# A Mamba-2 scan with top-1 experts on one core: sized second pass, transposes by DMA, and a respaced recurrence

## The chip, the cores and the metric

The kernel runs on one core of one Trainium2 chip. The metric is the device time of one execution in microseconds; the median of three runs of the kernel before is 324.8 us (323.02 to 328.04). The profile is of one execution with a span of 323.2 us from first to last instruction. Engines are called TensorE (PE, its weight loads PEld), VectorE (DVE), ScalarE (ACT), GpSimd (POOL) and SyncE (SP).

## The reference

Two parts follow one another. The first is a chunked state-space scan over 4 batches, 8 heads, 768 positions, head size 32 and state size 16:

```python
for c in range(nc):                                   # chunks of 32 in the reference
    cum = np.cumsum(log(clip(a, 1e-6, 1))[..., chunk], axis=-1)
    M = (C @ B.T) * exp(cum_i - cum_j) * causal
    y = M @ x + (C @ state) * exp(cum)
    state = exp(sum) * state + sum_j(exp(cum_last - cum_j) * B_j x_j)
```

The result, laid out as 3072 tokens of 256 numbers, goes through eight experts, one per token:

```python
logits = x @ w_gate                     # 3072 x 8
e = argmax(logits); gate = max(softmax(logits))
out[t] = gate[t] * (relu(x[t] @ w1[e]) @ w2[e])       # w1 256x1024, w2 1024x256
```

All is float32. The inputs are drawn with a fixed seed.

## The kernel before

**Recurrence.** The scan uses chunks of 64. A step `n` (24 of them, `NT`) is one chunk of two batches, a tile of 128 tokens. The loop over `n` is a pipeline of three: step `n` gets its decays (`a_rows` on TensorE, `decay`, a scan on VectorE), its scores (`scores`) and their weighing (`weigh`); step `k = n-1` gets its own state (`own`), the faded state (`fade`, `state`) and `y`; step `j = n-2` is turned into token rows with the eight logits (`rows`, a matmul with `turn` and a ScalarE copy). `scaled_B` and the decayed C (`ctd`, in `decay_in`) are made on GpSimd. The order on each engine is the order in which the Python calls stand: the schedule is written by hand.

**Routing.** Rows are collected in groups (`RGS`, five of 6, 6, 4, 4 and 4 tiles). For a group, `choose` finds the best expert and the one-hot (VectorE), `rank_pe` counts with small matmuls how many tokens of the same expert stand ahead, `rank` makes of it a row number in the table `x_hbm`, `gate_sum` and `gate` the softmax weight, which is stored in the row beside the token number. `place` scatters 128 rows by an indirect DMA from GpSimd, two calls a step. Each expert has a region in `x_hbm`; `empty` fills its first 448 rows with zeros and the token number N, which the last scatter drops. The first three groups (`GA`) may be read by the first pass; tokens of later groups stand behind row 256 (`CA`).

**Experts.** The first pass takes 256 rows of each expert, the second 192 more (`CB`): one full tile of 128 and a half tile of 64, two experts' halves sharing one tile (`m_half`). `m_load` reads rows, `xT_of` and `m_xT` transpose them on TensorE with VectorE copying the result, `m_h` makes the hidden layer (8 blocks of 128, ScalarE's ReLU evicting), `m_y` the output, `put` scales by the gate and scatters to `out`. The order is one hidden layer ahead: hidden of unit `u`, output of unit `u-1`. If any expert had more than 448 tokens, `general` would run; it doesn't with these inputs.

**Loads.** SyncE's queue issues them in program order. `load(g)` brings CT, BT, B and x for four steps into three rotating buffers; the weights of four experts (`EW`) are loaded in the loop, one matrix every second step from step 8, the rest during the first experts. The last eight tiles are placed in a row during the first pass, in front of the reads of the second.

Of the kernel before, what the change touches and what calls it, by code (L numbers as in the profile page):

```python
# [11 lines left out]
I32 = mybir.dt.int32  # L12
AX = mybir.AxisListType.X
# [7 lines left out]
CH = 64  # L21
# [5 lines left out]
RGS = [6, 6, 4, 4, 4]  # L27
GA = 3
# [4 lines left out]
GATE, TOK = DM + E, DM + E + 1  # L33
W = DM + E + 2
# [5 lines left out]
EW = 4  # L40
# [3 lines left out]
def ssd_then_moe(ctx, tc, x, ad_in, az_in, B, BT, CT, w_gate, w1, w2, out):  # L44
# [11 lines left out]
    ld = att.enter_context(tc.tile_pool(name="ld", bufs=3))  # L56
# [18 lines left out]
    zrows = sm.tile([112, CAP // 112, W], FP32, name="zrows")  # L75
# [13 lines left out]
    nk = route.tile([128, 2 * E + 1], I32, name="nk")  # L89
    spare = route.tile([1, 1], FP32, name="spare")  # L90

    def wake():

        z = sm.tile([128, 512], BF16, name="wake")
        nc.vector.memset(z, 0.0)
        p = ps.tile([128, 512], FP32, name="wake_ps", tag="rows", bufs=1)
        for _ in range(13):
            nc.tensor.matmul(p, lhsT=z[:, 0:128], rhs=z, start=True, stop=True)
# [22 lines left out]
    def late_consts(hs):  # L121
        for c in (slice(0, CG), slice(CG, NC)):
            nc.scalar.copy(hsel[:, c], bc(hs[:, c, :, None], list(hsel[:, c].shape)))
            if c.start == 0:
                nc.scalar.copy(selx[:, 2:2 * NC], bc(sel[:, 2:2 * NC, None], [128, 2 * NC - 2, CH]))

    def route_consts():
        nc.scalar.copy(turn[:, 0:128], ident)
        nc.scalar.copy(turn[:, 128 + 2 * E:], ident)
        nc.gpsimd.memset(cnt[:, 0, :], 0.0)  # L130
        nc.gpsimd.memset(cnt[:, GA + 1, :], 0.0)

        nc.gpsimd.memset(zrows, 0.0)
        none_i = sm.tile([112, CAP // 112], I32, name="none_i")
        nc.gpsimd.iota(none_i, pattern=[[0, CAP // 112]], base=N, channel_multiplier=0)
        nc.gpsimd.tensor_copy(zrows[:, :, TOK].bitcast(I32), none_i)
        nc.gpsimd.memset(Tmat, 1.0)
        nc.gpsimd.affine_select(out=Tmat, in_=Tmat, pattern=[[1, 128]], base=-1, channel_multiplier=-1,
                                compare_op=ALU.is_ge, fill=0.0)
        nc.gpsimd.memset(ones_bf, 1.0)  # L140
        iota_i = sm.tile([128, E], I32, name="iota_i")
        nc.gpsimd.iota(iota_i, pattern=[[1, E]], base=0, channel_multiplier=0)
        nc.gpsimd.tensor_scalar(out=rev_e, in0=iota_i, scalar1=-1.0, scalar2=float(E), op0=ALU.mult, op1=ALU.add)
        nc.gpsimd.tensor_scalar(out=base_f, in0=iota_i, scalar1=float(NR), scalar2=None, op0=ALU.mult)
        nc.gpsimd.tensor_scalar(out=base_e, in0=iota_i[0:1], scalar1=float(NR), scalar2=None, op0=ALU.mult)
        for s in range(2):
            nc.gpsimd.iota(tok_i[64 * s:64 * s + 64, :].rearrange("p (b c) -> p b c", b=NP),
                           pattern=[[2 * S, NP], [CH, NC]], base=S * s, channel_multiplier=1)

    def empty(e):  # L150
        nc.sync.dma_start(out=x_hbm[e * NR:e * NR + CAP, :].rearrange("(p c) w -> p c w", c=CAP // 112), in_=zrows)
# [15 lines left out]
    def split_az(eng, p, t):  # L167

        z = azp[p]
        f = t.rearrange("p h i -> p (h i)")  # L170

        def first():
            clip(eng, t)
            eng.memset(t[:, :, 0:1], 0.0)
        return [first,
                lambda: eng.tensor_copy(z, f),
                lambda: eng.tensor_tensor(out=f, in0=f, in1=z, op=ALU.subtract),
                lambda: eng.tensor_copy(z[32:64], f[32:64]),
                lambda: eng.tensor_copy(z[64:96], f[64:96]),
                lambda: eng.tensor_tensor(out=f[64:96], in0=f[64:96], in1=z[64:96], op=ALU.subtract),  # L180
                lambda: eng.tensor_copy(z[64:96], f[64:96])]

    def load(g):
        p, c0 = divmod(g * CG, NC)
        r = gr[g]
        T = CG * 128
        sl = slice(c0 * 128, c0 * 128 + T)
        r["CT"] = ld.tile([128, T], FP32, name="ct")
        nc.sync.dma_start(out=r["CT"], in_=CT[p, :, sl])
        r["BT"] = ld.tile([128, T], FP32, name="bt")  # L190
        nc.sync.dma_start(out=r["BT"], in_=BT[p, :, sl])
        r["B"] = ld.tile([128, CG, 128], FP32, name="bn")
        nc.sync.dma_start(out=r["B"], in_=B[p, :, c0:c0 + CG, :])
        r["x"] = ld.tile([128, CG, DM], FP32, name="xn")
        nc.sync.dma_start(out=r["x"], in_=x[p, :, c0:c0 + CG, :])

    def load_w(i):
        e, u = divmod(i, 2)
        nc.sync.dma_start(out=w_sb[e][u], in_=(w1, w2)[u][e])

    def masks(g):

        m = wk.tile([128, CG, 2, 2, CH], FP32, name="ctm")
        for u in range(2):
            nc.scalar.mul(m[:, :, :, u, :], gr[g]["CT"].rearrange("p (c s i) -> p c s i", c=CG, s=2), par[:, u:u + 1])
        gr[g]["ctm"] = m
# [6 lines left out]
    def decay_rows(t):  # L213

        d1 = sm.tile([128, NP * 2, CH], FP32, name="d1")
        nc.gpsimd.memset(d1, 0.0)
        clip(nc.gpsimd, t)
        nc.gpsimd.tensor_copy(d1[:, :, 0:1], t[:, :, 0:1])
        nc.gpsimd.memset(t[:, :, 0:1], 0.0)
        f = sm.tile([128, NP * 128], FP32, name="adf")  # L220
        nc.vector.tensor_tensor_scan(out=f, data0=t.rearrange("p h i -> p (h i)"),
                                     data1=d1.rearrange("p h i -> p (h i)"), initial=0.0, op0=ALU.mult, op1=ALU.add)
        return f

    def decay_split(f, ii):
        for i in ii:
            nc.gpsimd.tensor_copy(adp[i], f)
            if i < 2:
                nc.gpsimd.tensor_tensor(out=f, in0=f, in1=adp[i], op=ALU.subtract)
# [7 lines left out]
    def decay_in(ns, bank):  # L237
        for i, n in enumerate(ns):
            p, c = divmod(n, NC)
            for u in range(3):  # L240
                nc.tensor.matmul(bank[:, i], lhsT=hsel[:, c].rearrange("p h m -> p (h m)"),  # L241
                                 rhs=adp[u][:, 128 * p:128 * p + 128], start=(u == 0), stop=(u == 2),
                                 skip_group_check=True)
        for i, n in enumerate(ns):
            s = st[n]
            s["dec"] = wk.tile([128, 128], FP32, name="dec", bufs=4)
            nc.scalar.copy(out=s["dec"], in_=bank[:, i])  # L247
            s["ctd"] = wk.tile([128, 128], FP32, name="ctd", bufs=4)
# [3 lines left out]
    def a_rows(n):  # L252
        p, c = divmod(n, NC)
        t = ps.tile([128, 512], FP32, name="abc", bufs=2)
        nc.tensor.matmul(t, lhsT=selx[:, 2 * c:2 * c + 2].rearrange("p c j -> p (c j)"), rhs=azp[p],
# [11 lines left out]
    def scaled_B(n):  # L267
        nc.gpsimd.tensor_tensor(out=bs[n % 2], in0=gr[n // CG]["B"][:, n % CG].rearrange("p (h m) -> p h m", h=8),
                                in1=bc(st[n]["L"][:, :, CH - 1:CH], [128, 8, NS]), op=ALU.mult)

    def scores(n):
        c = n % CG
        g = ps.tile([128, 2, 512], FP32, name="g", bufs=1)
        for s in range(2):
            for t in range(2):
                for v in range(2):
                    r = slice(64 * t + 32 * v, 64 * t + 32 * v + 32)
                    o = c * 128 + s * CH
                    nc.tensor.matmul(g[64 * t:64 * t + 64, v, 128 * s:128 * s + 128],  # L279
# [15 lines left out]
    def own(k):  # L295
# [5 lines left out]
        for s in range(2):  # L301
            for t in range(2):
                for v in range(2):
                    r = slice(64 * t, 64 * t + 64)
                    h = 4 * s + 2 * v
                    nc.tensor.matmul(A[32 * (2 * t + v):32 * (2 * t + v) + 32, 0, 64 * s:64 * s + 64],  # L306
# [30 lines left out]
    def y(k):  # L337
# [3 lines left out]
        if inter:  # L341
            for s in range(2):
                for t in range(2):
                    for v in range(2):
                        r = slice(64 * t + 32 * v, 64 * t + 32 * v + 32)
                        o = s * CH
                        nc.tensor.matmul(p[64 * v:64 * v + 64, t, s * CH:s * CH + CH], lhsT=carry[k][r, s],  # L347
                                         rhs=st[k]["ctd"][r, o:o + CH], start=(s == 0), stop=False,
                                         skip_group_check=True)
        for s in range(2):  # L350
            for q in range(4):
                for t in range(2):
                    r = slice(64 * t, 64 * t + 64)
                    o = (4 * s + q) * D
                    nc.tensor.matmul(p[D * q:D * q + D, t, s * CH:s * CH + CH], lhsT=xk[r, o:o + D],  # L355
# [9 lines left out]
    def rows(k):  # L365

        p = ps.tile([128, DM + E], FP32, name="rows_ps", tag="rows", bufs=1)
        for t in range(KT):
            nc.tensor.matmul(p[:, 128 * t:128 * t + HB], lhsT=st[k]["yT"][:, t], rhs=turn[:, HB * t:HB * t + HB],  # L369
# [9 lines left out]
    def choose(g):  # L379
        n = RGS[g]  # L380
        sl = slice(R0[g], R0[g] + n)
# [6 lines left out]
        ex = route.tile([128, RG, E], FP32, name="ex")[:, 0:n]  # L388
        nc.scalar.activation(ex, sub, func=ACT.Exp)
# [3 lines left out]
                                       op0=ALU.is_equal, op1=ALU.mult)  # L393
        m2 = route.tile([128, RG], FP32, name="m2")[:, 0:n]
        nc.vector.tensor_reduce(m2, eq, axis=AX, op=ALU.max)
        nc.vector.tensor_tensor(out=oh_all[:, sl, :], in0=eq, in1=bc(m2[:, :, None], sh), op=ALU.is_equal)
        cs = route.tile([128, E], FP32, name="cs")
        nc.vector.tensor_reduce(cs, oh_all[:, sl, :].rearrange("p k e -> p e k"), axis=AX, op=ALU.add)
        nc.gpsimd.tensor_tensor(out=cnt[:, ci(g) + 1, :], in0=cnt[:, ci(g), :], in1=cs, op=ALU.add)
        rt_ex[g] = ex  # L400

    rt_ex, rt_se = {}, {}

    def gate_sum(g):
        n = RGS[g]
        se = rt_se[g] = route.tile([128, RG], FP32, name="se", bufs=2)[:, 0:n]
        nc.vector.tensor_reduce(se, rt_ex[g], axis=AX, op=ALU.add)
        nc.gpsimd.tensor_scalar_add(se, se, 1e-9)
        nc.gpsimd.tensor_copy(rt[g][:, :, TOK].bitcast(I32), tok_i[:, R0[g]:R0[g] + n])

    def gate(g):
        nc.vector.reciprocal(rt[g][:, :, GATE], rt_se[g])
# [3 lines left out]
    def rank_pe(g, p):  # L416
# [4 lines left out]
        nc.tensor.matmul(q, lhsT=ones_bf, rhs=bc(cnt[:, ci(g):ci(g) + 1, :], [128, n, E]), start=True, stop=False,  # L421
# [100 lines left out]
    def m_h(u, mo, pp, between):  # L522
# [3 lines left out]
        for f in range(FT):  # L526
            p = up(ex[u]["xT"][:, :, 0:n], w_sb[e][0], f, n, pp)
            nc.scalar.activation(ex[u]["hT"][:, f, 0:n], p, func=ACT.Relu)  # L528
            if f == FT // 2:
                between()  # L530
# [247 lines left out]
```

## Time and profile before

| what | us |
|---|---|
| median of three runs | 324.8 |
| span of the profiled run | 323.2 |
| TensorE busy | 289.2 (89%) |
| ScalarE busy | 105.0 (32%) |
| GpSimd busy | 92.1 (29%) |
| VectorE busy | 79.1 (24%) |
| first expert matmul starts | 112.49 |
| last matmul of TensorE ends | 316.6 |
| DMA moved | 39.93 MB |

How to read it: the busy shares are means over two very different halves. Up to 112 us the small matmuls of the recurrence alternate with work of all other engines; from there the expert matmuls run. The strip of 40 slices (8 us each) shows it:

```profile
PE   6679688788687899999999996999999999999991
PEld 2457466666565788888888885889999799798870
DVE  6937555753546522000000000010010010000000
ACT  5635334342243333223231412132233123332310
POOL 5874457235453100202111282102111101211121
PEclk9979787985689899999999999999999999999997
DMA  7969386936435693071720134100001101100000
```

Each digit is the busy share of a slice in tenths; PEclk is the clock that TensorE was granted.

### The profile page before, as it was taken

To read this page: it belongs to the slowest core of one execution; us is meant where nothing else is said; L and a number is where in the kernel's file an instruction comes from. 1 tells how busy PE (TensorE), PEld (TensorE's weight loads), DVE (VectorE), ACT (ScalarE), POOL (GpSimd) and SP (SyncE) were. 2 spreads that over 40 slices of the span, in tenths; PEclk is the share of its full clock that TensorE was granted. 3 is DMA by queue.
4 is the path that set the end of the run, shared out by engine and by line. 5 is a ranking of instruction groups with operands and counts; after the bars stand their busy time and mean duration, and the time that the engine had idled before them with its cause. 6 is when DMAs were issued, how large, how long until landed. Compare 5 with 4: busy or idle time off the path is not lost.

```text
span 323.2 us, 7506 instructions
## 1 busy us (share of the span) xinstructions
PE 289.2 (89%) x3150; PEld 241.2 (75%) x3172; DVE 79.1 (24%) x198; ACT 105.0 (32%) x292; POOL 92.1 (29%) x191
## 2 busy tenths in 40 slices
PE   6679688788687899999999996999999999999991
PEld 2457466666565788888888885889999799798870
DVE  6937555753546522000000000010010010000000
ACT  5635334342243333223231412132233123332310
POOL 5874457235453100202111282102111101211121
PEclk9979787985689899999999999999999999999997
DMA  7969386936435693071720134100001101100000
GB/s 229 355 201 306 130 308 200 315 130 199 113 103 163 257 370 153 31 291 38 290 68 16 50 118 131 33 13 34 0 32 47 36 0 53 43 18 2 19 16 31
DMA packets 13867, 39.93 MB, mean 124 GB/s; under 512 B 2299, under 2 KB 6014, under 8 KB 11776
## 3 DMA queue, kind: packets, MB, share of 16 engines
q1 hardware_dynamic: 11328, 32.94, 30.0%
q0 software_dynamic: 2496, 6.42, 5.5%
q8 instruction: 27, 0.44, 0.6%
q14 instruction: 16, 0.13, 0.1%
HBM read 29.12 MB, written 10.75 MB: 123 GB/s over the span
## 4 chain that ended last, share of the span: by engine, by line
PE 68%; issue 17%; POOL 5%; ACT 3%; DVE 3%; another core or an unknown queue 2%; DMA 1%; POOLq 0%; ACTq 0%
PE h_ps L519 23%; PE y_ps L546 20%; PE rows_ps L369 5%; PE g L279 5%; PE y L355 4%; POOL out_dram L535 3%; PE y L347 3%; PE A L306 2%; PE xT_ps L499 2%; PE A L241 1%; PE y_ps L556 1%; ACT rows L372 1%; DMA az<-in_az_dram 1%; POOL ctd L250 1%
## 5 line engine op out<-in xcount | busy, mean ns | idle before, releaser
L519 PE MATMUL h_ps<-xT,w 128*128 128x256 f32 (+1 forms) x512 | 102.6, 354 | 3.0 <-ACT hT L528 2.5
L519 PEld LDWEIGHTS h_ps<-xT,w 128*128 128x128 f32 x512 | 89.5, 190 | 11.4 <-ACT hT L528 3.2
L546 PE MATMUL y_ps<-w,hT 128*128 128x256 f32 x384 | 85.3, 379 | 0.0
L546 PEld LDWEIGHTS y_ps<-w,hT 128*128 128x128 f32 x384 | 72.7, 190 | 9.5
L528 ACT ACTIVATE hT<-h_ps 128x256 f32<-128x256 f32 (+1 forms) x128 | 45.5, 358 | 58.4 <-PE h_ps L519 53.6
L509 DVE COPY xT<-xT_ps 128x256 f32<-128x256 f32 x24 | 9.4, 420 | 158.2 <-PE xT_ps L499 158.2
L535 POOL DMA_INDIRECT out_dram<-yo,xs x16 | 15.7, 983 | 88.1 <-ACT yo L534 87.5
L263 DVE TENSOR_TENSOR_SCAN L<-abc,ident 128x512 f32<-128x512 f32 x24 | 29.0, 1210 | 0.0
L453 POOL DMA_INDIRECT x_hbm<-rows,pos x24 | 23.9, 995 | 12.5 <-issue 10.2
L535 POOL DMA_INDIRECT out_dram<-yo,xb x8 | 7.8, 974 | 58.7 <-ACT yo L534 50.1
L534 ACT ACTIVATE yo<-y_ps,xs 128x256 f32<-128x256 f32 x16 | 7.6, 474 | 48.8 <-PE y_ps L546 45.7
L279 PE MATMUL g<-ctm,bt 32*64 32x128 f32 x384 | 21.3, 321 | 1.8 <-issue 1.7
L369 PE MATMUL rows_ps<-turn,yT 128*128 128x136 f32 x96 | 18.8, 328 | 4.6 <-issue 3.1
L288 DVE TENSOR_TENSOR M<-g,L 128x512 f32<-128x512 f32 x24 | 16.6, 691 | 21.3 <-PE g L279 21.1
L355 PE MATMUL y<-M,xn 64*32 64x64 f32 x768 | 16.1, 246 | 5.1 <-issue 4.9
L369 PEld LDWEIGHTS rows_ps<-turn,yT 128*128 128x128 f32 x96 | 18.1, 234 | 1.5 <-ACT rows L372 0.3
L279 PEld LDWEIGHTS g<-ctm,bt 32*64 32x64 f32 x384 | 13.1, 152 | 7.6 <-issue 4.3
L372 ACT COPY rows<-rows_ps 128x264 f32<-128x264 f32 x24 | 9.1, 380 | 27.7 <-PE rows_ps L369 25.3
L250 POOL TENSOR_TENSOR ctd<-ct,dec 128x128 f32<-128x128 f32 x23 | 10.4, 458 | 23.8 <-ACT dec L247 22.4
L355 PEld LDWEIGHTS y<-M,xn 64*32 64x32 f32 x768 | 9.7, 118 | 9.1 <-issue 7.1
L359 ACT COPY yT<-y 128x256 f32<-128x256 f32 x24 | 8.9, 373 | 22.0 <-PE y L355 15.9
L556 PE MATMUL y_ps<-w,hT 128*64 128x256 f32 x128 | 14.7, 382 | 0.0
(127 smaller groups left out, 196.0 us busy)
## 6 DMA issues: line engine op xcount, KB each, us to landing
w<-in_w_dram SPq DMA_DIRECT2D x16, 1024.0 KB, 7.1
x_hbm<-zrows SPq DMA_DIRECT2D x8, 465.5 KB, 6.3
xn<-in_x_dram SPq DMA_DIRECT2D x6, 512.0 KB, 7.0
xs<-x_hbm SPq DMA_DIRECT2D x8, 266.0 KB, 3.7
ct<-in_CT_dram SPq DMA_DIRECT2D x6, 256.0 KB, 4.7
bt<-in_BT_dram SPq DMA_DIRECT2D x6, 256.0 KB, 6.6
bn<-in_B_dram SPq DMA_DIRECT2D x6, 256.0 KB, 5.7
xb<-x_hbm SPq DMA_DIRECT2D x8, 133.0 KB
```

The source lines that it names most:

```text
L250: nc.gpsimd.tensor_tensor(out=s["ctd"], in0=gr[n // CG]["CT"][:, o:o + 128], in1=s["dec"], op=ALU.mult)
L263: nc.vector.tensor_tensor_scan(out=s["L"].rearrange("p h i -> p (h i)"), data0=s["abc"], data1=ident8.rearrange("p h i -> p (h i)"), initi ...
L279: nc.tensor.matmul(g[64 * t:64 * t + 64, v, 128 * s:128 * s + 128], lhsT=gr[n // CG]["BT"][r, o:o + CH], rhs=gr[n // CG]["ctm"][r, c, s].r ...
L288: nc.vector.tensor_tensor(out=s["M"].rearrange("p (s v u) i -> p s v (u i)", s=2, v=2), in0=s["g"][:, :, 0:256].rearrange("p v (s f) -> p ...
L355: nc.tensor.matmul(p[D * q:D * q + D, t, s * CH:s * CH + CH], lhsT=xk[r, o:o + D], rhs=st[k]["M"][r, 4 * s + q], start=(not inter and s == ...
L369: nc.tensor.matmul(p[:, 128 * t:128 * t + HB], lhsT=st[k]["yT"][:, t], rhs=turn[:, HB * t:HB * t + HB], start=(t == 0), stop=(t == KT - 1) ...
L453: s_ = nc.gpsimd.indirect_dma_start(out=x_hbm[:, :], out_offset=bass.IndirectOffsetOnAxis(ap=pos[:, k:k + 1], axis=0), in_=rt[grp[k]][:, k ...
L519: nc.tensor.matmul(p[:, 0:n], lhsT=w[:, c:c + 128], rhs=xT[:, t], start=(t == 0), stop=(t == KT - 1))
L528: nc.scalar.activation(ex[u]["hT"][:, f, 0:n], p, func=ACT.Relu)
L535: s_ = nc.gpsimd.indirect_dma_start(out=out[:, :], out_offset=bass.IndirectOffsetOnAxis(ap=xs[:, TOK:TOK + 1].bitcast(I32), axis=0), in_=y ...
L546: nc.tensor.matmul(p, lhsT=ex[u]["hT"][:, f, 128 * t:128 * t + 128], rhs=w_sb[e][1][:, f * DM:f * DM + DM], start=(f == 0), stop=(f == FT ...
L556: nc.tensor.matmul(p[64 * i:64 * i + 64, :], lhsT=ex[u + i]["hT"][:, f, 128:CB], rhs=w_sb[e + i][1][:, f * DM:f * DM + DM], start=(f == 0) ...
```

## The change

Its parts, in the order of the program:

- **Start.** `split_az` of the first pair works by halves on VectorE and ScalarE together; the decays of the second pair of batches (`decay_ready`, `decay_rows`, `decay_split`) are made later, at steps 3 to 9. The constants of routing are spread over steps 2 to 5, the zero rows are made on ScalarE at step 12.
- **Loads.** All six groups have buffers of their own. From group 2 on, loads and the weights of one and a half experts are sent in threes, each batch tied to the matmul at which TensorE's count of passes reaches `99 + 253 * sent / 2`: behind TensorE's entry into the next block of its instructions. The other weights come during the first pass.
- **Routing.** Seven groups (2, 3, 3, 3, 3, 3, 7); 17 tiles belong to the first pass. `choose` is split, `rank_pe` comes a step later and stands among the matmuls of its step. The gate is no longer stored: `gate_in` and `gate_out` make it from the loaded logits. From step 6 on, one scatter a step. `empty` runs at the end, from a row number read into a register, and fills the 448 rows behind the first pass's tokens.
- **Seam.** `keep_on` puts two matmuls of zeros in front of the last rows; the last rows use another PSUM bank; expert 0 is turned on TensorE as before, its copies shared by VectorE and ScalarE, and its first block is split by 128 columns.
- **Turning.** For all other experts, `halves` splits the 32-bit rows into their 16-bit halves (VectorE), one DMA transpose on SyncE's queue turns them, `words` puts the halves together (VectorE).
- **Second pass.** Experts go in pairs. `over` also makes a class 0 to 4 for each pair from its larger count; TensorE and ScalarE read it into registers and choose one of five programs of 128, 144, 160, 176 or 192 columns; the program of class 0 has no half tile. Hints name the program ahead of each switch. Results are scaled on VectorE.
- **Late tiles.** The last seven tiles are placed one by one between the results of the first pass.

The core of it:

```diff
-RGS = [6, 6, 4, 4, 4]
-GA = 3
+RGS = [2, 3, 3, 3, 3, 3, 7]
+GA = 6
-EW = 4
+EW = 2
...
+    passes, sent, batches = [0], [0], []
+    def mm(out, lhsT, rhs, **kw):
+        i = nc.tensor.matmul(out, lhsT=lhsT, rhs=rhs, **kw)
+        passes[0] += 2 if rhs.dtype == FP32 else 1
+        if batches and passes[0] >= 99 + 253 * sent[0] // 2:
+            sent[0] += 1
+            for send in batches.pop(0):
+                d = send()
+                tc.add_manual_dep(d.ins, i.ins.name,
...
     def empty(e):
-        nc.sync.dma_start(out=x_hbm[e * NR:e * NR + CAP, :].rearrange("(p c) w -> p c w", c=CAP // 112), in_=zrows)
+        r = nc.values_load(row2[0:1, e:e + 1], engines=[ENG.SP], min_val=e * NR, max_val=e * NR + R0[GA] * 128,
+        d = nc.sync.dma_start(out=x_hbm[ds(r, CAP), :].rearrange("(p c) w -> p c w", c=CAP // 112), in_=zrows)
...
     def place(k):
-        nc.gpsimd.memset(spare, 0.0)
...
+        ml = tb.tile([128, E // 2], FP32, name="ml")
+        nc.vector.tensor_reduce(ml, cn.rearrange("p (b i) -> p b i", i=2), axis=AX, op=ALU.max)
+        nc.vector.tensor_scalar(out=ml, in0=ml, scalar1=float(15 - CA - 128), scalar2=0.0, op0=ALU.add, op1=ALU.max)
+        nc.vector.tensor_scalar(out=ml, in0=ml, scalar1=64.0, scalar2=None, op0=ALU.min)
+        cl = nk[:, 2 * E + 1:]
+        nc.vector.tensor_copy(cl, ml)
+        nc.vector.tensor_scalar(out=cl, in0=cl, scalar1=4, scalar2=None, op0=ALU.logical_shift_right)
...
+    def halves(tiles):
+        n = len(tiles)
+        pl = ea.tile([128, TA + 1, 2, KT, 128], U16, name="pl", bufs=2)[:, 0:n]
+        for i, xs in enumerate(tiles):
+            f = xs.bitcast(U16).rearrange("p (j c) -> p c j", c=2)
+            for t in range(KT):
+                nc.vector.tensor_copy(pl[:, i, :, t], f[:, :, HB * t:HB * t + 128])
+        tt = ea.tile([128, TA + 1, 2, KT, 128], U16, name="plT", bufs=2)[:, 0:n]
+        nc.sync.dma_start_transpose(out=tt.rearrange("p i c t j -> p (i c t) j"),
+                                    in_=pl.rearrange("p i c t j -> p (i c t j)"))
...
+    def words(xT, tt):
+        nc.vector.tensor_copy(xT.bitcast(U16).rearrange("p t (j c) -> p c t j", c=2), tt)
...
-            for _ in range(2):
-                if todo:
-                    place(todo.pop(0))
+            if todo:
+                place(todo.pop(0))
...
+        for v in range(E // 2):
+            pr[v]["hT"] = [new_hT(mo) for _ in range(2)]
+            for h in pr[v]["hT"]:
+                nc.vector.memset(h[:, :, 144:CB], 0.0)
+            for c in tc.Switch(cls[v], 5, f"p{v}"):
+                for i in range(2):
+                    m_h(2 * v + i, pr[v]["xT"][i], pr[v]["hT"][i], 128 + 16 * c, pp)
+                if c:
+                    m_half(v, mo, pp)
+            send(yh, pr[v]["xh"][:, 0])
+            if v + 1 < E // 2:
+                tc.switch_hint(cls[v + 1], 5, f"p{v + 1}")
+                b_words(v + 1)
+                b_gates(v + 1)
+                next_halves(E + v + 2)
+            for i in range(2):
+                m_y(2 * v + i, pr[v]["hT"][i][:, :, 0:128], pr[v]["xs"][:, i],
+                    pr[v]["gate"][:, i:i + 1], mo, pp, None, False, (v, i) == (E // 2 - 1, 1))
```

## The prediction

> **What bounds the kernel now.** I read the core's span and clock first (one core, 323.2 us, mean clock 0.941), then the strip of 40 slices, then busy times by stage, and last the chain and the order of time inside each stage.
>
> The cuts of the stage table are at the starts of step 2's first matmul, the first expert matmul, the end of the first pass's last down-projection, and the end of TensorE's work:
>
> ```profile
> 0.00:17.93 17.93, 10.99 (x191) 6.01 (x193) 12.20 (x24) 10.66 (x23) 12.55 (x44) 1.00 0.84 292
> 17.93:112.49 94.56, 76.70 (x1877) 58.25 (x1898) 53.74 (x126) 35.37 (x112) 43.12 (x100) 0.82 0.61 202
> 112.49:235.50 123.01, 120.47 (x585) 106.16 (x586) 9.44 (x37) 34.36 (x88) 23.77 (x34) 1.00 0.30 109
> 235.50:316.62 81.12, 81.02 (x499) 70.81 (x497) 3.73 (x12) 24.12 (x69) 11.69 (x12) 1.00 0.09 27
> ```
>
> Columns: stretch, length, busy TensorE, weight loads, VectorE, ScalarE, GpSimd, granted clock, DMA share, GB/s. From 112 us on TensorE is full at clock 1.00: only less matmul work shortens it. In the recurrence (rows 1 and 2) TensorE is busy 81% of the time at clock 0.82, and nothing else is full: there waits, and the clock that follows them, set the time.
>
> In order of time, TensorE around one routing group and, in the same listing for another window, one pair of scatters:
>
> ```profile
> 29.99 0.63 PE L369 MATMUL rows_ps<-turn,yT 128*128 128x136 f32 x4 [0.16 <-issue]
> ...
> 33.84 0.33 PE L355 MATMUL y<-M,xn 64*32 64x64 f32 x10 [1.84 <-issue]
> ...
> 37.21 0.28 PE L427 MATMUL rank<-oh_all,ones_bf 128*128 128x40 bf16 x5 [0.85 <-DVE oh_all L396]
> ...
> 39.74 1.13 PE L279 MATMUL g<-ctm,bt 32*64 32x128 f32 x16
> ...
> 43.86 0.67 PE L279 MATMUL g<-ctm,bt 32*64 32x128 f32 x16
> ```
> ```profile
> 71.92 1.01 PE L279 MATMUL g<-ctm,bt 32*64 32x128 f32 x7
> 73.23 0.55 PE L279 MATMUL g<-ctm,bt 32*64 32x128 f32 x6 [0.29 <-issue]
> 73.98 0.69 PE L279 MATMUL g<-ctm,bt 32*64 32x128 f32 x3 [0.20 <-issue]
> ```
>
> Three losses show: a stall that nothing explains while DMA was at 1.03 of its share (1.84 us), rank matmuls that wait for VectorE's one-hot, and, at 71.9 to 74.7, sixteen score matmuls that take 2.8 us instead of 0.67 while GpSimd issues two row scatters (71.16 and 72.54). After a stall the same matmuls run at half speed (1.13 against 0.67). The rows matmuls start at 24.38, 27.17, 29.99: an undisturbed step is 2.8 us. From 21.07 to 105.45 there are 19 steps in 84.38 us, 4.44 each: 31 us over the undisturbed rate.
>
> From the chain that ended last:
>
> ```profile
> 181.66 0.44 PE xT_ps L499 x4
> ...
> 184.69 6.91 PE y_ps L546 x32
> ...
> 193.27 3.84 another core or an unknown queue
> ...
> 235.50 3.25 PE h_ps L519 x20
> ...
> 253.47 3.60 PE y_ps L556 x32
> ```
>
> A 256-column matmul record costs 6.91/32 = 216 ns, a 192-column one 3.25/20 = 162.5, a 128-column one (a transpose) 0.44/4 = 110: time follows the columns, about 0.845 ns each. The half tiles cost 3.60 us a pair. At 193.27 ScalarE stood still and TensorE with it, 4.3 us until the path moved.
>
> **What the Trainium skill says.** "TensorE: Matmul & The Clock Gate", Part 1: an idle window of about 3.4 us halves the array's clock. The trace agrees: 0.50 in the two-microsecond stretches from 36 to 42, after the stalls. "Runtime: NRT & Kernel Launch", Instruction fetch mechanics: instructions come by DMA in blocks of 256, and a taken branch to a block not at hand waits for that fetch. The instruction queues' 27 packets of 0.44 MB, 16 KB each, fit the first part; no branch on TensorE's path is in the trace. "VectorE: DVE Perf Modes", The three transpose paths: 1309 ns for one 128x128 2-byte transpose by DMA. "Advanced Engine Details and Errata", X-Bar Transpose (TRN2): such transfers are about as fast as others, 350 to 400 GB/s. No run shows either yet.
>
> **Start.** The constants of routing leave the stretch 13.53 to 17.0 on GpSimd, where a scaled C and B waited behind them; TensorE stood 2.90 us. They are spread over steps 2 to 5, and the split of `a` and the decays are halved: 0.5 more. Step 2 starts at 14.5 instead of 17.93.
>
> **Recurrence.** The matmuls of a step stay: 2.8 us. Seventeen tiles in groups of 2 or 3 instead of sixteen in groups of 6, 6, 4 add rank matmuls, five per group at some 0.1 us: 0.2 a step. VectorE's fixed work is 1.21 (scan) + 0.69 (weigh) + 2 x 0.24 (state) = 2.4 us; seven small routing operations of 0.19 us a group add 0.44 a step, so 2.8: under TensorE's 3.0, which I take as the step. The rank matmuls now come a step after the one-hot, so their wait (0.47 + 0.85 four times, plus a cold stretch each, in all some 13 us of the 31) goes: by the same count 4.2 (34.92 to 44.68), 3.0 (57.64 to 69.05), 3.1 and 2.6 (100.52 to 108.73). ScalarE (2.0 a step) and GpSimd (0.4 + 0.46 + 1.0 + counts, 2.4) lie under this. Loads leave three at a time, 768 KB per 126 passes of TensorE, about 2 us of DMA per 4 us, which leaves the fetch room: of the 1.84 us stall I keep 1. Six of eight expert weight transfers no longer fall here.
>
> The scatters are the unknown. From rows to rows over 2.8 a step, the stretches with scatters lose 4.6 (44.68 to 57.64), 5.1 (69.05 to 79.76), 3 of 6.2 (79.76 to 91.58) and 3.3 (91.58 to 100.52): about 16 us of the 31 for sixteen scatters, cold clock included, 1.0 each. One per step from step 6 instead of two back to back: at best 0.2, at worst 1.0 each; I take 0.6, so 17 x 0.6 = 10 us. The end keeps its 7.0 us from 105.45 to the first expert matmul, less 0.5 for the seam. Sum: 14.5 + 2.5 (first matmul to rows) + 19 x 3.0 + 10 + 1 + 6.5 = 91.5 for the first expert matmul, before 112.5.
>
> **First pass.** Sixteen blocks of 6.91 are 110.6. Seven transposes of 0.44 (3.1 us) go to DMA. The 4.3 us stop came while eight scatters ran back to back (184.30 to 194.1) in front of two result scatters; now there is one between results, so I drop it. The added waits: VectorE now waits for the transposed halves, and behind it only the next expert's copies and gates are queued; TensorE needs them one expert (13.8 us) later. A transposition moves 256 KB: by the bandwidth 0.7 us and about 3 with its landing (loads here take 3.7 us), by the single price 8 x 1.309 = 10.5. Both fit 13.8, except expert 1, due 6.9 us after the first matmul, and expert 2, whose rows are emptied and loaded first. I take 4 us per transposition and 2 us of stall in all; 5 + 3 at the worst price. VectorE's copies (about 4 us per 14) and ScalarE's exponentials lie under the matmuls; so do the weight loads, 2 MB per 13.8 us, 7 us to land. First pass: 112.6, ending at 204.1.
>
> **Second pass.** The reference's inputs are seeded; I counted its choices: with 17 tiles in pass one the experts leave 116, 102, 162, 161, 106, 119, 159, 150 places beyond 256. A pair's class comes from its larger one over 128, in sixteens: 0, 3, 0, 2, so 128, 176, 128 and 160 columns, and class 0 drops the half tiles. Before, each pair: 2 x 5.20 + 2 x 3.45 + 3.60 + 0.66 for transposes = 21.6, in all 86.2. After: class 0: 64 x 0.110 + 6.9 = 13.9, twice; class 3: 64 x 0.149 + 3.6 + 6.9 = 20.0; class 2: 64 x 0.136 + 10.5 = 19.2. Sum 67.1, 19.1 less.
>
> A switch costs a jump in and one out, on TensorE and ScalarE, with hints given 6.9 us ahead (before a pair's down-projections) and at each program's start. Branches themselves are 51 to 108 ns by the skill ("Advanced Engine Details and Errata", Control Flow Timing). If a hint fails, a fetch costs what stalls of this trace cost, 1.84 to 3.87 us, eight times. I take 0.6 a switch, 2.5 us. The registers are read in the middle of a down-projection; queued behind each read are TensorE's remaining matmuls, and earlier ones already sent should cover it: nothing. Second pass 69.6, ending at 273.7.
>
> **Tail.** 6.6 us as before (316.62 to 323.20): scaling on VectorE instead of ScalarE (0.47), one scatter (0.97), landing. Span 280.3; the median time stands 1.6 above the span: 282.
>
> **Rivals.** (a) The scatters cost as before, 1.0 each (+7), VectorE's routing chain makes the step 3.2 (+4), branches 1 us (+2): 295. For it: matmuls slow down while GpSimd issues. Against: the slow stretches were pairs of scatters. (b) Hints fail and transpositions come at the single price: 8 x (1.84 to 3.87), say 23, + 6 over my stalls: 311. For: no trace shows either. (c) Slower than before: a transposition of eight blocks takes longer than an expert. At 2.2 us a block, 17.6 and 26.4 for a pair: 7 x 3.8 + 4 x 9.6 = 65 us: 347. Against: both prices of the skill. (d) Scatters spread out cost 0.2 and switches and stalls nothing: 282 - 7 - 4.5 = 270.
>
> **Chances.** The forecast 0.55 (274 to 290), (a) 0.20, (b) 0.08, (c) 0.06, (d) 0.11. The range takes in (d), the forecast and (a) with its unknown: 266 to 306; (b) and (c) stay out, 0.14. Everything but (c) is over 2% faster; with little between: faster 0.92, no difference 0.02, slower 0.06.
>
> **What would show it.** Right: first expert matmul near 91 us; rank without a VectorE wait; recurrence clock above 0.9; no transposes on TensorE but expert 0's; second pass near 70 us with 128-, 176-, 128- and 160-column matmuls. Wrong: VectorE's halves copy waiting on DMA into TensorE's idle time; gaps of 2 to 4 us at the four switches; score and y matmuls still in bursts at every scatter.

## The result, and the profile after

The changed kernel takes 271.8 us (median of three runs, 271.16 to 272.35) against 324.8 before; the ratio is 0.839, with an interval of 0.832 to 0.846. The forecast was 282. The profiled span is 270.0 us, mean granted clock 0.992 (before 0.941). A few executions of the kernels below fell in a slower state of the chip; the medians leave them out, and of the profiles only that of `m1_static` is of one.

The stage table of the changed kernel, cut at the same events as the one of before (step 2's first matmul, first expert matmul, end of the first pass, end of TensorE's work, where the cut lies 0.2 us early: its last matmul ends at 262.76; columns as there):

```profile
0.00:14.13 14.13, 11.48 (x195) 6.23 (x201) 9.95 (x25) 11.29 (x25) 8.44 (x34) 1.00 0.85 281
14.13:83.20 69.07, 62.00 (x1880) 48.89 (x1902) 55.88 (x131) 39.86 (x119) 43.55 (x99) 1.00 0.57 171
83.20:194.56 111.36, 111.36 (x527) 97.81 (x528) 27.03 (x131) 32.47 (x88) 22.07 (x24) 1.00 0.72 223
194.56:262.56 68.00, 67.83 (x449) 60.78 (x447) 17.39 (x71) 20.92 (x72) 11.74 (x12) 1.00 0.20 40
262.56:270.00 7.44, 0.20 (x1) 0.00 (x0) 0.48 (x1) 0.00 (x0) 1.16 (x2) 0.72 0.08 25
```

The first expert matmul moved from 112.49 to 83.20: 29.3 us. In row 2 TensorE does practically the same matmuls as before (1880 against 1877) in 62.0 instead of 76.7 busy microseconds, since its clock is 1.00 instead of 0.82, and idles 7.1 instead of 17.9. The two expert passes together shrank from 204.1 to 179.4: 24.8 us (they are not compared singly: the kernel before computes one hidden layer of the second ahead of the cut between them). TensorE is busy in every microsecond of the first. The tail gave back 0.9. Together 53.2, the difference of the two spans.

What TensorE waited for in the recurrence of the changed kernel, two of the longer waits (us in total, times, longest; the pauses at the rows matmuls, 0.3 at most, are left out):

```profile
PE y L176 <- issue: 1.4, 4, 0.5
PE xT_ps L632 <- DMA xs<-x_hbm: 0.9, 1, 0.9
```

and before:

```profile
PE y L355 <- issue: 4.9, 9, 1.8
PE rank L427 <- DVE oh_all L396: 3.5, 4, 0.9
```

The rank matmuls' wait for the one-hot is gone, and unexplained stalls of the `y` matmuls fell from 4.9 to 1.4. At the start, the wait for the scaled B (`bs`) shrank; before and after:

```profile
PE A L306 <- POOL bs L268: 3.5, 2, 2.9
PE A L176 <- POOL bs L366: 0.5, 1, 0.5
```

The second pass in the chain that ended last (start, length):

```profile
194.56 7.14 PE h_ps L685 x64
...
208.61 9.55 PE h_ps L685 x64
218.17 3.60 PE yh_ps L731 x32
...
228.88 7.14 PE h_ps L685 x64
...
242.93 0.17 issue
243.10 8.95 PE h_ps L685 x64
```

Pairs one and three have 128 columns and no half tile, two 176, four 160; the only gap at a switch is 0.17.

One table serves most experiments: the start of the second rows matmuls, the 19 steps from there to the 21st, the stretch from there to the first expert matmul, and TensorE's busy and idle time from the first rows matmuls to that expert matmul. All in us, from the traces; the median is that of the runs. Runs of one kernel scatter by about 1 us (271.16 to 272.35 for the changed one), so smaller differences between medians say nothing.

| kernel | second rows | 19 steps | seam | busy | idle | median |
|---|---|---|---|---|---|---|
| before | 21.07 | 84.38 | 7.04 | 77.3 | 20.8 | 324.8 |
| changed | 16.73 | 59.05 | 7.42 | 62.6 | 7.1 | 271.8 |
| `s1_pairs` | 16.40 | 67.44 | 6.25 | 65.2 | 11.5 | 279.6 |
| `s2_spare` | 16.22 | 59.61 | 7.13 | 62.8 | 6.8 | 272.4 |
| `s3_loads` | 17.91 | 62.36 | 7.61 | 63.6 | 11.0 | 276.2 |
| `s4_rank` | 16.56 | 67.13 | 6.25 | 63.6 | 13.0 | 278.4 |
| `s5_three` | 17.72 | 81.95 | 6.25 | 71.2 | 21.4 | 293.6 |
| `b1_single` | 22.33 | 77.07 | 8.81 | 72.1 | 20.3 | 320.7 |
| `c1_seam` | 16.48 | 60.20 | 6.98 | 62.9 | 7.1 | 272.3 |

### The profile page after: what moved, and what is told of

Read it like the earlier page. It is cut to its first block, busy times and chain, and to the rows that moved or that the text cites. A ratio compares the mean times of both kernels' runs of the same rounds, so it can differ in the third digit from the quotient of the medians.

```text
span 270.0 us, 7603 instructions
## 1 busy us (share of the span) xinstructions
PE 252.9 (94%) x3044; PEld 213.7 (79%) x3067; DVE 110.7 (41%) x358; ACT 104.5 (39%) x304; POOL 87.0 (32%) x171
## 4 chain that ended last, share of the span: by engine, by line
PE 82%; DVE 5%; DMA 4%; issue 4%; POOL 2%; ACT 1%; POOLq 0%; ACTq 0%; DVEq 0%
PE h_ps L685 33%; PE y_ps L720 30%; PE y L176 5%; PE rows_ps L176 4%; PE g L176 3%; PE A L176 3%; PE yh_ps L731 3%; DVE L L359 2%; DMA x_hbm<-rows,pos 1%; DMA xs<-x_hbm 1%; DMA az<-in_az_dram 1%; DMA ct<-in_CT_dram 1%; DVE M L386 1%; PE rank L176 1%; DVE S L431 1%
## 5 line engine op out<-in xcount | busy, mean ns | idle before, releaser
L685 PE MATMUL h_ps<-xT,w 128*128 128x256 f32 (+3 forms) x516 | 90.3, 334 | 0.6 <-ACT xT L641 0.5
L685 PEld LDWEIGHTS h_ps<-xT,w 128*128 128x128 f32 x516 | 81.3, 190 | 8.2 <-ACT xT L641 0.7
L696 ACT ACTIVATE hT<-h_ps 128x256 f32<-128x256 f32 (+3 forms) x128 | 43.3, 339 | 60.8 <-PE h_ps L685 53.1
L711 POOL DMA_INDIRECT out_dram<-yo,xs x24 | 23.7, 988 | 91.1 <-ACT yo L703 64.7
L651 DVE COPY pl<-xs 128x256 uint16<-128x256 uint16 x44 | 10.4, 298 | 43.8 <-DMA xs<-x_hbm 43.7
L658 DVE COPY xT<-plT 128x512 uint16<-128x512 uint16 (+1 forms) x30 | 10.6, 415 | 33.6 <-DMA plT<-pl 27.8
L703 ACT ACTIVATE yo<-y_ps,gate 128x256 f32<-128x256 f32 x14 | 6.6, 474 | 39.4 <-PE y_ps L720 24.5
L386 DVE TENSOR_TENSOR M<-g,L 128x512 f32<-128x512 f32 x24 | 16.5, 687 | 5.6 <-PE g L176 5.1
L705 DVE TENSOR_SCALAR yo<-y_ps,gate 128x256 f32<-128x256 f32 x10 | 4.8, 482 | 29.3 <-PE y_ps L720 29.3
L176 PE MATMUL g<-ctm,bt 32*64 32x128 f32 x384 | 16.3, 280 | 0.5 <-ACT ctm L293 0.4
L366 POOL TENSOR_TENSOR bs<-bn,L 128x128 f32<-128x128 f32 x22 | 9.0, 410 | 11.1 <-DVE L L359 10.0
```

Source lines behind the costliest of these rows:

```text
L176: i = nc.tensor.matmul(out, lhsT=lhsT, rhs=rhs, **kw)
L386: nc.vector.tensor_tensor(out=s["M"].rearrange("p (s v u) i -> p s v (u i)", s=2, v=2), in0=s["g"][:, :, 0:256].rearrange("p v (s f) -> p ...
L651: nc.vector.tensor_copy(pl[:, i, :, t], f[:, :, HB * t:HB * t + 128])
L658: nc.vector.tensor_copy(xT.bitcast(U16).rearrange("p t (j c) -> p c t j", c=2), tt)
L685: nc.tensor.matmul(p[:, i:min(i + step, n)], lhsT=w[:, c:c + 128], rhs=xT[:, t, i:min(i + step, n)], start=(t == 0), stop=(t == KT - 1))
L696: nc.scalar.activation(hT[:, f, 0:n], p, func=ACT.Relu)
```

## Experiments on the recurrence

The question: which part made the 19 steps 25.3 us shorter, and do scatters cost by their number or by their spacing?

**Pairs.** `s1_pairs`:

```diff
-            if todo:
-                place(todo.pop(0))
+            if len(todo) > 1 or n > 20:
+                for j in range(2):
+                    if todo:
+                        if j:
+                            nc.gpsimd.memset(spare, 0.0)
+                        place(todo.pop(0))
```

> The changed kernel with its scatters issued two back to back (as soon as two are waiting, with a small GpSimd memset between them) instead of one a step; same number of scatters, all else alike. Theory T1 (two scatters in a row slow TensorE's small matmuls for some 2 us, a single one hardly does): eight pairs, 8 to 14 us slower than the changed kernel, and score or y matmuls of 2 us and more behind each pair. Rival T2 (not the spacing but other work, such as the loads, made the stretches with scatters slow): no change, 0 to 1 us.

Measured 279.6 us, 7.7 more (ratio to before 0.862, 0.854 to 0.870). TensorE's and then GpSimd's order around one pair:

```profile
49.78 0.63 PE L176 MATMUL rows_ps<-turn,yT 128*128 128x136 f32 x4 [0.16 <-issue]
52.21 0.43 PE L176 MATMUL A<-xn,bs 64*32 64x64 f32 x16 [1.80 <-issue]
```
```profile
49.41 1.03 POOL L553 DMA_INDIRECT x_hbm<-rows,pos  x1 [0.50 <-issue]
...
50.75 0.96 POOL L553 DMA_INDIRECT x_hbm<-rows,pos  x1 [0.21 <-issue]
51.73 0.42 POOL L366 TENSOR_TENSOR bs<-bn,L 128x128 f32<-128x128 f32 x1
```

The `A` matmuls read the scaled B, `bs`. It stands behind both scatters on GpSimd and is done at 52.15; `A` starts at 52.21. The profile puts the 1.80 us down to "issue", yet the two times and the operand show a wait for `bs`. After it the clock falls: its records show half speed from 53.05 to 56.47, and the rows here are cut at these times.

```profile
49.64:53.05 3.41, 1.47 (x28) 1.21 (x29) 2.55 (x6) 1.56 (x5) 3.02 (x7) 1.00 0.56 159
53.05:56.47 3.42, 3.09 (x70) 2.68 (x72) 1.10 (x5) 1.15 (x3) 2.58 (x7) 0.50 0.48 166
```

"TensorE: Matmul & The Clock Gate", Part 1, of the Trainium skill puts the drop after an idle window of about 3.4 us; here a stretch of 3.41 us with 1.47 us of work in it was enough for half the clock.

This wait stands at one pair of eight. From rows to rows its step took 6.06 us (49.78 to 55.84), 2.5 more than the same step of the changed kernel. More of the loss lies in smaller stops. Around another pair, TensorE and GpSimd:

```profile
35.12 0.32 PE L176 MATMUL y<-M,xn 64*32 64x64 f32 x10
35.80 0.32 PE L176 MATMUL y<-M,xn 64*32 64x64 f32 x5 [0.36 <-issue]
36.56 0.42 PE L176 MATMUL y<-M,xn 64*32 64x64 f32 x17 [0.45 <-issue]
```
```profile
33.73 1.03 POOL L553 DMA_INDIRECT x_hbm<-rows,pos  x1 [0.16 <-issue]
...
35.07 0.96 POOL L553 DMA_INDIRECT x_hbm<-rows,pos  x1 [0.22 <-issue]
```

The `y` matmuls are broken by ten such gaps without a releaser, 4.1 us in all, after six of the eight pairs. Nine of them end 0.6 to 1.5 us after the second scatter of a pair began. The six steps are 0.3 to 1.7 us longer than those of the changed kernel, 6.0 together. The changed kernel has four such gaps (1.4 us); three end 1.3 us after one of its seventeen scatters began. So the gaps go with the scatters and are more frequent behind pairs. They are not the wait for `bs`, which these matmuls don't read; what causes them stays open. Spacing it is, not number: theory T1 holds, a little under its lower bound, and T2 falls.

**The memset.** `s2_spare` puts `nc.gpsimd.memset(spare, 0.0)` back ahead of each scatter.

> The changed kernel with the memset of one spare element that the kernel before has ahead of every scatter put back (24 of them). If the memset was what made the scatters cost 1 us each in the kernel before: 8 us or more slower. If it was the spacing: within 1 us of the changed kernel.

Measured 272.4 us (ratio 0.839, 0.833 to 0.844): no difference.

**Spacing in the kernel before.** `b1_single`:

```diff
-            for _ in range(2):
+            for _ in range(2 if n >= 20 else 1):
```

> The kernel before with one scatter a step instead of two until step 20, all else as it was. If the spacing acts alone, it gains here what pairing lost in the changed kernel: 6 to 9 us faster than the kernel before. If the other waits of that recurrence keep the scatters' cost hidden or in place: under 3 us.

Measured 320.7 us, 4.5 less than the 325.3 of the kernel before beside it (ratio 0.984, 0.977 to 0.992), between the two ranges expected. The 19 steps are 7.3 shorter, nearly the 8.4 that pairing costs there in the changed kernel. But the second rows, ahead of any scatter, came 1.3 later in this profile, and the seam is 1.8 longer, with a wait of 1.57 for the first expert's rows.

**Loads.** `s3_loads`:

```diff
-                d = send()
-                tc.add_manual_dep(d.ins, i.ins.name,
...
+                send()
```

> The changed kernel with its bulk loads still in threes and in the same places of SyncE's program, but no longer tied to matmuls: they leave as soon as SyncE's queue takes them. Theory T4 (bulk loads delay the instruction blocks, and the tie keeps them apart): 6 to 10 us slower, with stalls of 1 to 4 us in TensorE's time that no other engine explains, during the first 60 us. T1 (the tie is of little weight beside the spacing of the scatters): 0 to 2 us slower.

Measured 276.2 us, 4.4 more (ratio 0.851, 0.845 to 0.858), between the two theories. Nearly all of it is lost before 34 us:

```profile
16.43 0.34 PE L176 MATMUL y<-ctd,S 32*64 32x64 f32 x8 [1.59 <-issue]
...
21.23 0.67 PE L176 MATMUL g<-ctm,bt 32*64 32x128 f32 x16 [1.28 <-DMA bt<-in_BT_dram]
...
31.97 0.34 PE L176 MATMUL y<-M,xn 64*32 64x64 f32 x15 [1.44 <-issue]
```
```profile
13.31:17.91 4.60, 2.85 (x87) 2.23 (x88) 2.65 (x7) 2.00 (x7) 2.30 (x11) 1.00 1.05 387
...
25.00:33.58 8.58, 6.15 (x178) 4.80 (x180) 5.88 (x17) 5.29 (x15) 6.91 (x18) 0.93 0.99 335
```

While DMA stands at 1.0 of its share, TensorE stalls three times for more than a microsecond. With the tie the share is 0.36 to 0.76 in this stretch and none of the three stalls is there. Two have no releaser, like the 1.84 us in the kernel before. The profile puts the third down to a tile of `BT`, but these matmuls are step 4's, the first of the second group of loads, whose `BT` was issued at 5.05 and had landed 5.3 us later. So it is a stall of the same kind, and so is one of 0.50 us at 26.48.

The records of the trace say more. The four stalls stand 251, 244 and 243 passes of TensorE apart, counted as `mm` counts them (some records are missing); two batches of the tie are 253 apart. Each stall ends 1.3 to 1.8 us after a packet of 16 KB of the instruction queue has ended: 15.02, 19.47, 25.20 and 30.45. In the changed kernel these packets end at 13.81, 17.29, 21.25 and 25.35, and TensorE doesn't stop. Bulk loads that delay the blocks of TensorE's instructions, as theory T4 has it, fit all of this; no run changes the fetches alone.

**One-hot and rank in one step.** `s4_rank`:

```diff
                     if stage == 2:
+                        choose_max(q)
+                        choose(q)
+                        count(q)
                         rank_pe(q, ps.tile([128, RG + 1, E], FP32, name="rank", tag="rows", bufs=1))
```

with the same calls taken out of the earlier steps.

> The changed kernel with the one-hot, the counts and the rank matmuls of a group all in one step again, as in the kernel before: TensorE's rank matmuls then wait for VectorE's one-hot. By the prediction's sum (13 us for three of the five groups) six small groups give 8 to 15 us more, with waits of the rank matmuls on VectorE of 0.5 to 1.5 us each. If the wait was harmless once the step had slack: under 3 us.

Measured 278.4 us, 6.5 more (ratio 0.856, 0.849 to 0.863), under the range expected. The rank tile's own view of this kernel says what its engine sat idle for (us, times):

```profile
  DVE oh_all L499: 7.2, 6
```

Six groups wait 1.2 us each, and these waits are nearly the whole loss: 19 steps are 8.1 longer, and the seam 1.2 shorter. After the waits at 32.69 and 44.43 the clock fell, after the other four, among them 1.06 us at 55.40, it stayed at 1.00.

**All three undone.** `s5_three` is `s1_pairs`, `s3_loads` and `s4_rank` in one kernel.

> The changed kernel with three parts undone together: scatters in pairs, loads not tied to matmuls, one-hot and rank matmuls in one step. Alone they cost 7.7, 4.4 and 6.5 us. If they add up: 18.6 us slower, and the other 9 us by which the recurrence became faster come from other parts. If they compound (a stall of one leaves a slow clock and a full queue for the next): 22 to 28 us slower.

Measured 293.6 us, 21.7 more (ratio 0.898, 0.891 to 0.905), between the sum of 18.6 and the range of 22 to 28 for parts that compound. The 19 steps take 22.9 more, where 8.4 + 3.3 + 8.1 = 19.8 would be their sum. Alone each part adds 4 to 6 us of idle time but only 1.0 to 2.6 of busy time; together 14.3 and 8.6. So the idle times add up, and what exceeds the sum, 3.1 us, is busy time. The clock has a part in it:

```profile
13.30:105.92 92.62, 71.23 (x1885) 55.55 (x1905) 55.69 (x134) 39.98 (x120) 43.94 (x111) 0.91 0.37 129
```

Half speed lasts 17.1 us in the clock's records of this stretch, where the three alone have 3.4, 3.4 and 6.8; the 3.4 us more cost at most 1.7. The other 1.4 is open.

With 81.95 this recurrence is within 2.4 us of the 84.38 of before, so the three parts account for nearly all of the gain. It is not the recurrence of before, though: its rank matmuls wait for the one-hot six times (6.3 us), those of before four times (3.5), so how the gain divides among the three there isn't shown.

**The seam.** `c1_seam`: two scatters a step from step 20 on (`for j in range(1 if n < 20 else 2)`, with the memset between).

> The changed kernel with two scatters a step from step 20 on, so that the last row scatter of the first pass leaves earlier than 75.55 us. If TensorE's wait of 0.90 us for the first expert's rows comes from that last scatter's landing, it goes, and the first expert matmul stands 1.5 us behind the start of the last step's rows instead of 2.65: 0.9 to 1.1 us faster, less about 0.4 for each pair that now stands back to back. If the wait is the load's own, no change.

Measured 272.3 us (ratio 0.836, 0.831 to 0.841): no difference from the changed kernel. The end of the recurrence in its chain, below that of the changed kernel:

```profile
75.55 3.50 DMA x_hbm<-rows,pos
79.07 2.96 DMA xs<-x_hbm
```
```profile
74.00 3.75 DMA x_hbm<-rows,pos
77.77 4.73 DMA xs<-x_hbm
```

Each chain goes on with the first expert's transposes, at 82.08 and 82.54. The load left 1.3 us earlier and took 1.8 longer. Why, this trace doesn't settle. The seam without this wait is 6.25 (three runs of the table), so 1.2 us is all that could be had.

## Experiments on the expert passes

**No choice of programs, and a forced one.** `m1_static` has no switch, hint or class, and computes 192 columns for every pair; `m2_class4` keeps the switch and forces the class:

```diff
-            for c in tc.Switch(cls[v], 5, f"p{v}"):
+            for c in (4,):
```
```diff
-scalar1=float(15 - CA - 128), scalar2=0.0
+scalar1=1000.0, scalar2=0.0
```

> The changed kernel without the choice of programs: every pair of the second pass is computed at 192 columns with half tiles, and there is no switch, no hint and no class register. By columns alone: 2 x 64 x (0.1625 - 0.1116) + 3.6 twice for the two small pairs, 64 x (0.1625 - 0.1492) and 64 x (0.1625 - 0.1398) for the others: 6.5 + 7.2 + 0.9 + 1.5 = 16 us slower than the changed kernel, if switches cost nothing; up to 2.5 less (13.5) if they cost the 0.6 each that the prediction gave them.

> The changed kernel with the switch kept, but every class forced to 4 (192 columns), so that the work equals the one without a switch. The difference between the two is what four switches cost: 2.5 us if the prediction's 0.6 each holds, under 1 us if hinted switches cost no more than the one gap of 0.17 us that the trace shows.

Measured 288.0 (ratio 0.886, 0.879 to 0.893) and 288.3 us (0.886, 0.877 to 0.895): 16.1 and 16.5 more than the changed kernel. The chains of the two, first to last block of the second pass:

```profile
199.93 10.40 PE h_ps L685 x64
...
277.26 3.66 PE y_ps L720 x16
```
```profile
194.67 10.40 PE h_ps L685 x64
...
215.78 10.54 PE h_ps L685 x64
...
272.14 3.66 PE y_ps L720 x16
```

77.33 us without the switch, 77.47 with it: four switches cost 0.14 us, all in one block. The two traces differ by 5.2 us ahead of the first expert matmul (88.71 against 83.46), which has nothing to do with the switches; the other blocks of the second pass are equally long. The same stretch of the changed kernel is 255.66 - 194.56 = 61.10, so the sizing is worth 16.4.

**No hints.** `m3_nohint` takes the two `tc.switch_hint` lines out. Of the eight branch hints that TensorE's sequencer runs for the four switches, four go; the four that belong to the switch statement itself stay.

> The changed kernel without the hints ahead of the four switches. If a hint is what hides the fetch of the chosen program, each switch now shows a gap on TensorE of 1.84 to 3.87 us (one or two per switch): 7 to 15 us slower, and up to 31 at the prediction's rival of eight fetches. If the fetch is hidden by what TensorE has queued anyway: no change.

Measured 271.8 us (ratio 0.838, 0.830 to 0.845): no change. Of its second pass, the first, second and last blocks:

```profile
193.66 7.14 PE h_ps L685 x64
...
207.71 9.63 PE h_ps L685 x64
...
254.43 3.67 PE y_ps L720 x16
```

60.77 us against 61.10, and no gap at any switch. "Runtime: NRT & Kernel Launch", Instruction fetch mechanics, says that a taken branch to a page not at hand waits for its fetch. Fetches there were: in the second pass of `m1_static` and then of `m2_class4`, which computes the same with switches, the instruction queue of 16 KB packets has (packets, MB, share)

```profile
q8 instruction: 3, 0.05, 0.3%
q8 instruction: 10, 0.16, 1.0%
```

and 14 in the changed kernel, with and without the hints. They lay under TensorE's queued matmuls: each switch follows a block of 6.9 us, and at the second pair the sequencer of the changed kernel branches at 205.08, 3.4 us before the pair's first matmul. Without any hint at all, no run tells.

**The burst.** `m4_burst` places the seven late tiles in a row after the fifth expert's first result instead of one by one.

> The changed kernel with the seven late tiles scattered in one burst behind the fifth expert's first result instead of one by one between results. The kernel before stood still 4.3 us while such a burst ran. If the burst causes it (results wait behind the scatters on GpSimd until the ScalarE eviction has no free buffer): 3 to 6 us slower, with one idle gap of TensorE in the first pass. If the stop came from something else that the change removed (transposes and rows on other engines): no change.

Measured 272.6 us (ratio 0.838, 0.831 to 0.845). The scatters run back to back from 149.22 to 157.85, and TensorE's first pass has no gap:

```profile
83.92:195.44 111.52, 111.44 (x527) 97.81 (x528) 26.81 (x131) 32.48 (x88) 22.48 (x31) 1.00 0.72 222
```

So such a burst alone stops nothing in the changed kernel, and what else stopped ScalarE in the kernel before isn't shown. In `b1_single`, whose expert passes are those of before, that stop is 1.74 + 0.59 us of TensorE's time at the same place. Its cause stays open; the changed kernel also has other loads beside the burst.

**Transposes back on TensorE.** `m5_peturn` lets TensorE turn all experts (`nc.tensor.transpose` into a PSUM bank, one VectorE copy each) and leaves out `halves`, `words` and the DMA transposes.

> The changed kernel with the DMA transposes, the splitting into halves and the joining taken out again: TensorE turns all experts and VectorE copies the result. By the columns alone 7 x 4 x 0.11 + 4 x 6 x 0.11 = 5.7 us slower. More than 7: TensorE also waits for the copies. Under 4: the DMA transposes cost something in the changed kernel that its full TensorE row does not show.

Measured 277.3 us (ratio 0.856, 0.848 to 0.864), 5.5 more. In the profiled run, 4.6 above the changed kernel's, the expert passes take 5.7 more and the stretch ahead of them 0.9 less:

```profile
82.35:197.19 114.84, 114.84 (x561) 101.19 (x562) 18.04 (x90) 32.59 (x88) 21.86 (x24) 1.00 0.55 194
197.19:267.40 70.21, 70.09 (x466) 62.56 (x465) 14.89 (x59) 21.05 (x72) 11.74 (x12) 1.00 0.09 27
```

3.5 more in the first pass and 2.2 in the second, together the time of its 52 transposes (52 x 0.110 = 5.7). The DMA way costs nothing on the path: VectorE waits for turned halves 27.8 us in eight waits, 4.7 at most, and TensorE for none.

## Why the prediction was right, and where it missed

**Start.** Second rows at 17.0 predicted, 16.73 measured. The number is right, and the wait named, 2.90 us for GpSimd's scaled B, is gone; no run undoes this part alone.

**Recurrence.** The sum had 19 x 3.0 + 10 + 1 = 68; measured 59.05. The step of 3.0 fits: 59.05 / 19 is 3.1 with everything in it. The term that failed is "one per step from step 6 instead of two back to back: ... I take 0.6, so 17 x 0.6 = 10 us": with 57 for the steps only 2.05 is left for scatters and fetch together, at most 0.12 a scatter, just under the low end of 0.2. The error was to read the stretches of before, where scatters stand in pairs, as a cost of each scatter. Pairing costs 7.7, some 0.45 a scatter, and of the 8.4 in the 19 steps some 6.0 are small stops of TensorE behind six pairs, 2.5 the step in which the scaled B stood behind a pair. With one a step, `bs` is still in time. The rank term looks oversized: "some 13 us of the 31" for four waits and their cold stretches; undone alone, with six waits, it costs 8.1 in the 19 steps and 6.5 in all.

The reading that the trace of before agrees with an idle window of 3.4 us was not right: ahead of the 0.50 from 36 to 42 its longest idle time is 1.84 us. The conclusion that waits cost clock holds.

**Seam.** 6.5 predicted, 7.42 measured: the half microsecond of the seam was not gained, since the first expert's rows arrive 0.90 late.

**First pass.** 112.6 predicted, 111.36 measured. The stall term, 2 us, was zero; the transposes were hidden as forecast, and `m5_peturn` confirms their 5.7. "4 us per transposition" was 3.2 to 5.6 from issue to VectorE's copy, in the eight cases in which VectorE waited.

**Second pass.** 69.6 predicted, 68.0 measured. The columns came out as counted (67.1 of matmuls against 67.83 busy); "I take 0.6 a switch, 2.5 us" was 0.14 for four.

**Tail.** 6.6 predicted, 7.44 measured, 7.2 from the end of TensorE's last matmul. The last scatter now starts 1.4 us behind that matmul (262.76 to 264.15) instead of 0.85: GpSimd first copies one element to `spare` and then stands 0.63 us.

The errors by stage, measured less predicted: start -0.27, recurrence -8.95, seam +0.92, passes -2.84, tail +0.84, in all -10.3, which is 270.0 - 280.3. So the sign and the plan were right, the price of a scatter was not. The 271.8 us lie in the range of 266 to 306, but outside the forecast's own 274 to 290: the range held because it took in rival (d), scatters spread out at 0.2 with switches and stalls at nothing, which stood at 270 with a chance of 0.11. (a) falls with the 59.05 us and with `m2_class4`; (b) with the first pass and with switches of 0.14 us; (c) because TensorE waits for no turned half.

The gain by parts: start 4.3, recurrence 25.3 (22.9 for spacing, loads and rank together), sized programs 16.4, transposes 5.7, TensorE's idle time in the expert passes 2.5 (204.13 - 120.47 - 81.02, and 0.17 after), less 0.4 at the seam and 0.9 in the tail: 52.9 of 53.2. Experiments undo the three parts of the recurrence, the sizes and the transposes; the start and the idle time are read from the traces alone.

## What to carry to other kernels

A slow operation on an engine off the path can cost more in pairs than alone, so put one between two deadlines, not two. In part this was an operand that queued behind the pair; for the larger part here, TensorE's matmuls stopped behind it for reasons unknown. Look for the operand that waits, even where the profile says "issue", and check a releaser that it does name: one had landed ten microseconds before. Stalls of a microsecond can compound, in part through the clock, so undo suspects together as well as alone before blaming one. A choice among programs of several widths was nearly free here where a long block of matmuls preceded it.

## What the runs showed that was not expected

- A granted clock of 0.50 followed idle stretches of 1.4 to 1.8 us (`s1_pairs` at 52, `s4_rank` at 44, `s3_loads` at 32), while gaps of 1.59 and 1.28 us in `s3_loads` left it at 1.00. In the recurrence of these runs half clock lasted 3.41 us each time. Cut into stretches of that length, the stretch of `s3_loads` from 29.02 to 32.43 had 1.97 us of work and half the clock followed; the one from 18.78 to 22.19 had 1.97 too, and the full clock followed: busy time alone doesn't decide.
- Taking away the hints ahead of four five-way switches made no measurable difference: 60.77 us without, 61.10 with.
- An earlier load can land no earlier: 4.73 against 2.96 us for the same two transfers of 265 KB.
